# Soft-capped attention and soft mixture of experts on one core: polynomial exponentials on pairs of tiles

## The chip, the cores and the metric

The kernel runs on one core of one Trainium2 chip. The metric is the device time of one execution in microseconds; lower is better. The core has TensorE (PE) for matrix products, ScalarE (ACT) for tables such as exp and tanh, VectorE (DVE) for elementwise work, GpSimd (POOL) and SyncE (SP). In this kernel GpSimd casts v and issues the loads of weights, q and k; SP issues the loads of v and the stores of the output.

## What is computed

Attention over 8 batches of 12 heads, 448 tokens and head size 64, with scores capped by a tanh, and then a mixture of experts in which every token goes softly to 32 slots (8 experts with 4 slots each). Cut to what matters:

```python
scores = scale * np.matmul(q, k.transpose(0, 1, 3, 2))
scores = cap * np.tanh(scores / cap)
attn = np.exp(scores - max) / sum
x = np.matmul(attn, v)                      # then (3584, 768)

logits = x @ phi                            # 3584 x 32
d = softmax over tokens of logits
slot_input = d.T @ x                        # per expert 4 x 768
slot_out[e] = np.maximum(slot_input[e] @ w1[e], 0.0) @ w2[e]
out = softmax over slots of logits @ slot_out
```

cap is 30, so exp needs no subtraction of a maximum here; the kernel works without one.

## The kernel before

Two heads that lie beside each other in the array are a pair (48 pairs), two pairs a quad Q (24 quads, three to a batch of the input). A tile is 64 keys of both heads against 448 queries: 128 partitions by 448. Each pair has 7 tiles, 336 in all, and 6 tiles are a chunk j, 56 chunks. So one batch of the input is 7 chunks, and the main loop's pattern repeats every 7 chunks.

In chunk j ScalarE does two tanh over three tiles each (line 306, reading scores from PSUM) and one exponential over the tiles of chunk j-1 (line 310, in place). To relieve ScalarE, some tiles get their exponential on VectorE: poly_exp (lines 334 to 344) builds 2 to a power by a cubic polynomial in five steps. Step 0 scales to fixed point in int32 (line 337), step 1 shifts the whole part into the exponent of a bfloat16 (line 339), steps 2 to 4 are scalar-tensor-tensor instructions (lines 340 to 342) on the fraction. They use one work space, xe, xp and xb, of one tile's size. PARTS and EXTRA say for each chunk whether its first tile goes this way and in which slot of which chunk each step is issued; exp_chunk then leaves that tile out.

The order of every engine's queue is written by hand. The loop over j has slots named 0, e, a, b, r, c and d, between the fixed calls: tanh, exponential of the chunk before, the first part of a pair's product with v (pv_first), slot a, its tail, the scores of a coming half chunk (qk_chunk), slot b, the rest of the product and its normalisation (pv_rest with slot r, then norm: a reciprocal, line 367, and a multiplication, line 370), slot c, scores, slot d. A "<" or ">" puts a call at the start or end of a slot. WHEN places transposes of q and k, transposes of x, logits and sums; FILL places matmuls that compute nothing. A pair is normalised two chunks after its last tile.

PSUM is used in full: two buffers of three banks for scores (psS), one bank for the product (psV), one for all transposes and small sums (psT). So one slow reader in psV or psT holds PE up.

Other names that matter: vcast (272) casts a quad's v from vraw to one of two block-diagonal buffers vbd on GpSimd and then loads the next v. x_transp (415) turns one pair's x; logits (432) multiplies one quad's x with phi and adds the result into lg with VectorE; e_exp (448) takes the exponential of lg on ScalarE. wjobs (122) lists the loads of weights: w1, then the part of w2 that goes to DRAM as bfloat16 (w2d), then the part that stays (w2b, R2 blocks). After the attention, its pools are closed, and w2d is read back into the memory that they leave (w2t, lines 788 to 793). hpad, which holds the hidden layer with zeros around, takes the place of the work space.

## Time and profile before

| | |
|---|---|
| Median of 3 runs | 301.31 us (301.26 to 301.6) |
| The profiled execution | 301.64 us, span 299.9 us |
| ACT tanh, line 306 | 161.6 us busy, 113 instructions |
| ACT exponential, line 310 | 144.0 us busy, 58 instructions |
| DVE polynomial, lines 337, 339, 340, 341, 342 | 19.8, 18.2, 31.7, 33.6 and 29.9 us busy, 45 instructions each |
| DVE xT copies, line 419 | 17.9 us busy, 46 instructions |
| POOL casts of v, lines 275 and 276 | 21.7 and 25.3 us busy, 23 instructions each |
| PE fill, line 390 | 14.0 us busy, 244 instructions |
| w2t read back, line 792 | 20 transfers of 384 KB, 5.9 us to landing |
| Granted clock of TensorE | 0.988 of full, mean of the span |

The span is the time from the first to the last instruction of the profiled execution; the execution's own time is a little longer. Busy times of a row are sums of durations, and on ScalarE and VectorE the end of one instruction overlaps the start of the next, so starts are compared rather than durations where rates matter.

### The profile page before, as it was taken

What the parts mean: (1) busy time and instruction counts of PE and PEld (TensorE: products, weight loads), DVE (VectorE), ACT (ScalarE), POOL (GpSimd) and SP (SyncE); (2) the same over time, 40 slices, a digit from 0 to 9 for tenths busy, and PEclk for the clock granted to TensorE, in tenths of its full rate; (3) what the DMA queues carried; (4) which work ended last, traced back from release to release, by engine and by line L of the source; (5) the groups of instructions that cost most, each with busy time, mean ns of one, the idle gap of its engine ahead of it and who ended that gap; (6) DMA issues with size and microseconds to landing.
All of it is one profiled execution on the core that took longest, in us unless ns stands there. A gap on an engine that the chain in (4) does not pass through costs nothing.

```text
span 299.9 us, 10423 instructions
## 1 busy us (share of the span) xinstructions
PE 262.7 (88%) x4561; PEld 175.2 (58%) x4561; DVE 236.8 (79%) x511; ACT 268.0 (89%) x211; POOL 137.7 (46%) x179
## 2 busy tenths in 40 slices
PE   8898988998899989988998889998899999999830
PEld 7655656656665666565665666565666677642410
DVE  3728989888998999899988997999899974236850
ACT  3999999999999999999999999999999999136740
POOL 4493663395439525943393539453834232000000
PEclk9999999999999999999999999999999999999995
DMA  7999999699999999999989999999999749938997
GB/s 231 236 206 204 209 206 205 137 207 203 231 199 195 195 231 195 213 201 231 181 114 230 230 224 191 203 229 229 157 220 229 174 127 342 404 142 329 405 420 316
DMA packets 58061, 67.69 MB, mean 226 GB/s; under 512 B 3873, under 2 KB 54305, under 8 KB 58017
## 3 DMA queue, kind: packets, MB, share of 16 engines
q0 software_dynamic: 42448, 35.31, 76.2%
q1 hardware_dynamic: 15280, 31.50, 29.6%
q8 instruction: 35, 0.57, 0.7%
q10 hardware_dynamic: 288, 0.23, 0.3%
q14 instruction: 10, 0.07, 0.1%
HBM read 91.32 MB, written 18.87 MB: 367 GB/s over the span
## 4 chain that ended last, share of the span: by engine, by line
ACT 57%; PE 22%; DVE 13%; issue 3%; DMA 1%; POOL 1%; DVEq 0%; SPq 0%; ACTq 0%
ACT ex L306 32%; ACT ex L310 23%; PE pv L360 5%; PE sc L297 2%; DVE xq L370 2%; PE so_ps L843 2%; DVE ex L342 2%; PE hp L810 2%; DVE work L341 2%; DVE work L340 1%; ACT ob L935 1%; PE boot L618 1%; PE op L879 1%; PE op L926 1%; PE junk L615 1%
## 5 line engine op out<-in xcount | busy, mean ns | idle before, releaser
L306 ACT ACTIVATE ex<-sc 128x1344 bf16<-128x1344 f32 (+1 forms) x113 | 161.6, 1682 | 1.3 <-PE sc L297 1.3
L310 ACT ACTIVATE ex<-ex 128x2240 bf16<-128x2240 bf16 (+4 forms) x58 | 144.0, 2508 | 0.1
L360 PE MATMUL pv<-vbd,ex 128*128 128x130 bf16 (+1 forms) x1610 | 94.4, 211 | 10.6 <-DVE xq L370 5.5
L360 PEld LDWEIGHTS <-ex 128*128 128x128 bf16 (+1 forms) x1680 | 76.0, 101 | 31.6 <-issue 6.7
L297 PE MATMUL sc<-qT,kT 64*64 64x448 bf16 x672 | 69.8, 359 | 4.2 <-ACT ex L306 3.3
L275 POOL CAST vbd<-vraw 64x896 bf16<-64x896 f32 x23 | 21.7, 943 | 69.1 <-PE pv L360 40.9
L341 DVE SCALAR_TENSOR_TENSOR work<-work 128x448 f32<-128x448 f32 x45 | 33.6, 747 | 0.8
L456 POOL COPY e<-E 128x512 bf16<-128x512 bf16 x9 | 5.5, 613 | 60.0 <-ACT E L450 30.6
L340 DVE SCALAR_TENSOR_TENSOR work<-work 128x448 f32<-128x448 uint16 x45 | 31.7, 704 | 0.0
L297 PEld LDWEIGHTS <-kT 64*64 64x64 bf16 x672 | 24.7, 105 | 10.2 <-issue 6.8
L342 DVE SCALAR_TENSOR_TENSOR ex<-work 128x448 bf16<-128x448 f32 x45 | 29.9, 663 | 0.7
L370 DVE TENSOR_TENSOR xq<-pv,rec 128x448 bf16<-128x448 f32 x46 | 28.7, 624 | 1.6
L276 POOL CAST vbd<-vraw 64x896 bf16<-64x896 f32 x23 | 25.3, 1101 | 1.4
L115 POOL DMA_DIRECT2D w1b<-in_moe_w_dram x32 | 24.8, 777 | 0.0
L419 DVE COPY xT<-xps 128x448 bf16<-128x448 bf16 x46 | 17.9, 388 | 6.7 <-PE xps L413 6.2
L337 DVE TENSOR_SCALAR work<-ex 128x448 int32<-128x448 bf16 x45 | 19.8, 441 | 0.0
L267 DVE COPY kT<-kps 128x896 bf16<-128x896 bf16 x23 | 14.3, 622 | 6.3 <-PE kps L265 5.6
L339 DVE TENSOR_SCALAR work<-work 128x448 uint16<-128x448 uint16 x45 | 18.2, 404 | 0.5
L187 POOL DMA_DIRECT2D kb<-in_k_dram x22 | 16.1, 732 | 5.3 <-PE kps L265 4.7
L187 POOL DMA_DIRECT2D qb<-in_q_dram x22 | 16.2, 734 | 3.0 <-DMA kraw<-in_k_dram 3.0
L408 PE MATMUL xps<-ident,xq 128*128 128x128 bf16 x141 | 15.5, 219 | 1.7 <-DVE slacc L511 1.4
L367 DVE RECIPROCAL rec<-pv 128x7 f32<-128x7 f32 x46 | 9.3, 203 | 9.4 <-PE pv L360 8.8
(136 smaller groups left out, 346.3 us busy)
## 6 DMA issues: line engine op xcount, KB each, us to landing
w1b<-in_moe_w_dram POOLq DMA_DIRECT2D x32, 384.0 KB, 8.9
vraw<-in_v_dram SPq DMA_DIRECT2D x23, 448.0 KB, 6.2
w2d<-in_moe_w_dram POOLq DMA_DIRECT2D x20, 384.0 KB, 9.7
w2t<-w2d SPq DMA_DIRECT2D x20, 384.0 KB, 5.9
out_dram<-ob SPq DMA_DIRECT2D x7, 768.0 KB, 6.7
qb<-in_q_dram POOLq DMA_DIRECT2D x22, 224.0 KB, 9.2
kb<-in_k_dram POOLq DMA_DIRECT2D x22, 224.0 KB, 8.5
w2b<-in_moe_w_dram POOLq DMA_DIRECT2D x12, 384.0 KB, 8.8
```

The costliest lines, as they stand in the source:

```text
L115: pool.dma_start(out=w1b[e][:, js, fs], in_=w1r[:, e, js, fs])
L187: (sp if nm == "v" else pool).dma_start(out=t, in_=quad_ap(nm, Q))
L275: pool.tensor_copy(t[0:HP, :, :, 0:DH], raw[0:HP])
L276: pool.tensor_copy(t[HP:P, :, :, DH + 1:VW - 1], raw[HP:P])
L297: pe.matmul(sc[cs, u, 0:S], qkT["k", Q][r, c, cs], qkT["q", Q][r, :, cs], start=True, stop=True)
L306: act.activation(exs[j][:, half * CS + u0:half * CS + u1, :], sc[:, u0:u1, 0:S], ACT.Tanh, scale=qk_scale / cap)
L310: act.activation(exs[j][:, u0:u1, :], exs[j][:, u0:u1, :], ACT.Exp, scale=cap)
L340: lambda: dve.scalar_tensor_tensor(xp, frac, p2, frac, ALU.add, ALU.mult),
L341: lambda: dve.scalar_tensor_tensor(xp, xp, p1, frac, ALU.add, ALU.mult),
L342: lambda: dve.scalar_tensor_tensor(t, xp, p0, xb, ALU.add, ALU.mult))
L360: pe.matmul(out_, exs[j][r, u, q0:q0 + (HP if tail else P)], v_, start=(c == 0 and g == gs[0] < NF), stop=(c == NT - 1), skip_group_check= ...
L370: dve.tensor_tensor(xq[Q][:, h, s0:s1, :], pv[:, 0:s1 - s0, 0:DH], rec.to_broadcast([P, s1 - s0, DH]), op=ALU.mult)
```

## The change

The polynomial works on one or two tiles at once. The work space doubles, and xe, xp and xb are cut to the size that a call needs. In chunks 7 to 48, every second residue modulo 7 (0, 2, 4 and 6) now gives its first two tiles to VectorE; chunks 3 to 5 and 50 to 53 give one as before, chunks 6 and 49 none. All placings in PARTS, WHEN and FILL are new.

x is turned by quads with one copy instead of by pairs with two. The logits of a batch are formed in one go over all six parts in PSUM, and the small exponential reads them there; lg is gone, and the call moves to a new slot m between the two tanh. In the last batch the sum that identity matmuls brought in is formed by products directly.

v is loaded and cast in halves of 64 partitions. A half-cast follows directly after a pair's products; where the buffer itself would not make it wait, a memset of one element that is already zero does. 10 parts of w2 (of 4 blocks by half the columns) stay instead of 12, 22 go through DRAM instead of 20. The pools of the attention are laid out in the order in which they die, and hpad moves into the memory that they leave. Three of the first junk matmuls go.

```diff
-    R2 = 24
+    KEPT = 10
...
-    w2b = wts.tile([P, R2, D], BF16, name="w2b")
+    w2b = wts.tile([P, KEPT, 4, HD], BF16, name="w2b")
...
+    w2_parts = [(n0, half) for n0 in range(0, len(blocks), 4) for half in range(2)]
+    w2_kept, w2_spilled = w2_parts[:KEPT], w2_parts[KEPT:]
...
-    work = consts.tile([P, 5 * S // 2], I32, name="work", tag="work", bufs=1)
-    xe, xp, xb = work[:, 0:S], work[:, S:2 * S].bitcast(F32), work[:, 2 * S:].bitcast(BF16)
...
-    for nm in ("ex1", "ex2", "vb0", "ex3", "ex4", "ex0", "vb1"):
...
+    NP = 2
+    for nm in ("qk0", "ex1", "wk", "ldv", "ex2", "ex3", "vb0", "qk1", "ex4", "ex0", "vb1"):
+        homes[nm] = att.enter_context(tc.tile_pool(name=nm, bufs=1))
...
+    work = wk.tile([P, 5 * NP * S // 2], I32, name="work")
+    xe, xp = work[:, 0:NP * S], work[:, NP * S:2 * NP * S].bitcast(F32)
+    xb = work[:, 2 * NP * S:].bitcast(BF16)
...
+    vraw = ldv.tile([P, 2, S], F32, name="vraw")
+
+    def load_v(Q, n):
+
+        if Q < NQ:
+            r = slice(n * HP, n * HP + HP)
+            src = quad_ap("v", Q)
+            sp.dma_start(out=vraw[r],
+                         in_=bass.AP(tensor=src.tensor, offset=src.offset + n * S * DH,
+                                     ap=[[NT * DH, HP]] + list(src.ap[1:])))
+            raws["v", Q] = vraw
...
-    def vcast(Q):
-        raw = raws.pop(("v", Q)).rearrange("p h (c d) -> p h c d", d=DH)
-        t = vbds[Q % 2]
-        pool.tensor_copy(t[0:HP, :, :, 0:DH], raw[0:HP])
-        pool.tensor_copy(t[HP:P, :, :, DH + 1:VW - 1], raw[HP:P])
+    def vcast(Q, n):
+        raw = raws["v", Q].rearrange("p h (c d) -> p h c d", d=DH)
+        r, c0 = slice(n * HP, n * HP + HP), n * W
+        pool.tensor_copy(vbds[Q % 2][r, :, :, c0:c0 + DH], raw[r])
         if Q != 1:
-            load("v", max(Q + 1, 2))
+            load_v(max(Q + 1, 2), n)
+
+    def vcast_after(pr):
+
+        Q, h = divmod(pr, 2)
+        if h == 0 and 1 < Q + 1 < NQ:
+            pool.memset(vbds[Q % 2][HP:P, h, NT - 1, 0:1], 0.0)
+            vcast(Q + 1, 1)
+        elif h == 1 and Q + 2 < NQ:
+            vcast(Q + 2, 0)
...
+    PARTS = {0: (2, ((0, "a", (0,)), (1, "a", (1, 2)), (1, "c", (3,)), (1, ">d", (4,)))),
+             2: (2, ((0, "a", (0,)), (0, ">d", (1, 2)), (1, "a", (3,)), (2, "a", (4,)))),
+             4: (2, ((0, "a", (0,)), (0, ">b", (1,)), (0, ">d", (2,)), (1, "<b", (3,)), (1, ">d", (4,)))),
+             6: (2, ((0, "r", (0, 1)), (0, "<d", (2,)), (0, ">d", (3,)), (1, "<d", (4,))))}
+    shared = {j: (PARTS[j % 7],) for j in range(7, NCH - 8) if j % 7 in PARTS}
...
-    def poly_exp(j, u, ops):
-        t = exs[j][:, u, :]
+    def poly_exp(j, u, tiles, ops):
+        n1 = tiles * S
+        t = exs[j][:, u:u + tiles, :].rearrange("p u s -> p (u s)")
+        e, p, b = xe[:, 0:n1], xp[:, 0:n1], xb[:, 0:n1]
+        f, w = frac[:, 0:n1], whole[:, 0:n1]
...
-    def x_transp(pr, copy=dve.tensor_copy):
...
+    def x_transp(Q, hs=(0, 1), copy=dve.tensor_copy):
+        if Q not in xTs:
+            xTs[Q] = xs.tile([P, 2, S], BF16, name="xT", tag="xT", bufs=3)
+        ps = psT.tile([P, 2, S], BF16, name="xps", tag="T")
+        for h in hs:
+            turn_x(ps[:, h, :], 0, 2 * Q + h, range(NG))
+        copy(xTs[Q][:, hs[0]:hs[-1] + 1, :], ps[:, hs[0]:hs[-1] + 1, :])
...
-    def logits(Q, ps=None):
...
+    def logits(b):
+        lps[b] = psT.tile([P, NG, NS], F32, name="lps", tag="T")
         for g in range(NG):
...
+            for jt in range(NJ):
+                phi_mms(lps[b][:, g, :], xTs[b * NQB + jt // 2][:, jt % 2, :], g, jt,
+                        jt == 0, jt == NJ - 1)
...
-        act.activation(es[b], lgs.pop(b), ACT.Exp)
+        act.activation(es[b], lps.pop(b), ACT.Exp)
...
-    FILL = ((3, "a", fill, 2), (4, "a", fill, 2), (5, "a", fill, 2), (6, "a", spare, 10), (6, "c", spare, 12), (7, "a", fill, 18), (8, "a", fill, 8), (9, "a", fill, 2))
+    FILL = ((3, "a", fill, 16), (4, "a", fill, 10), (5, "a", fill, 8), (6, "a", spare, 10), (6, "c", spare, 14), (7, "a", fill, 12), (8, "a", fill, 16), (9, "a", fill, 4))
...
+    WHEN = {"k1": (0, "a"), "q1": (-1, "d"), "v1": (1, "c"), "k2": (2, "b"), "q2": (2, "d"), "v2": (4, "b"), "k3": (4, "b"), "q3": (5, "b"), "v3": (10, "b"), "x0": (5, "a"), "x1": (8, "d"), "x2": (10, "a"), "lg": (10, "d"), "ee": (11, "m"), "ss": (11, "d"), "et": (13, "a"), "en": (13, "b"), "es": (14, "c")}
...
-    busy(28)
+    busy(25)
...
         tanh_chunk(2 * j)
         if j == NCH - 1:
             exp_chunk(j - 1)
+        run(j, "m")
         tanh_chunk(2 * j + 1)
...
             pv_rest(pr, aux.pop((j, "r"), ()))
+            vcast_after(pr)
...
-    for s in range(2):
-        pe.matmul(lps[s], id32s[0], lg[:, 2 * s:2 * s + 2, :], start=True, stop=False,
-                  skip_group_check=True)
-    x_transp(last - 2)
+    x_transp(NQ - 2, (1,))
...
     for gs in ((0, 1, 2), (NF,)):
-        for pr in (last - 3, last - 2):
+        for pr in range(last - 5, last - 1):
             phi_last(pr, gs)
...
-    clear_hpad()
...
+    for n0, half in sorted(w2_spilled, key=lambda x: (x[1], x[0])):
+        t = tl.tile([P, 4, HD], BF16, name=f"w2t{n0}_{half}")
+        sp.dma_start(out=t, in_=w2d[n0, half])
+        w2t[n0, half] = t
+
+    hpad = tl.tile([P, E, NFT, NS], BF16, name="hpad")
+    pool.memset(hpad, 0.0)
```

## The prediction

> **What bounds the kernel now.** I read the page's shares first, then the chain, then the groups by shape, then the same five stretches for all engines, and last the timelines of ScalarE and VectorE inside one stretch. The page's first part and its chain:

> ```profile
> PE 262.7 (88%) x4561; PEld 175.2 (58%) x4561; DVE 236.8 (79%) x511; ACT 268.0 (89%) x211; POOL 137.7 (46%) x179
> ...
> ACT 57%; PE 22%; DVE 13%; issue 3%; DMA 1%; POOL 1%; DVEq 0%; SPq 0%; ACTq 0%
> ```

> Three engines are near 80 to 90%, so the mean does not decide. The main loop repeats every 7 chunks (one batch), and the exponential over all six tiles comes once in a batch, so its starts mark the period: 60.97, 91.77, 122.57, 153.37, 184.17 in the chain. That is 30.80 us each time. Busy times of the engines in these stretches:

> ```profile
> 60.97:91.77 30.80, 28.04 (x518) 19.16 (x516) 27.73 (x60) 30.80 (x23) 18.19 (x24) 1.00 1.15 207
> 91.77:122.57 30.80, 28.45 (x531) 19.59 (x528) 28.17 (x62) 30.80 (x23) 18.06 (x24) 1.00 1.16 205
> 122.57:153.37 30.80, 28.19 (x520) 19.32 (x519) 27.78 (x62) 30.80 (x24) 16.70 (x22) 1.00 1.12 196
> 153.37:184.17 30.80, 27.48 (x519) 19.04 (x519) 27.59 (x61) 30.80 (x24) 17.29 (x22) 1.00 1.20 206
> 184.17:214.97 30.80, 27.13 (x514) 18.86 (x511) 28.38 (x59) 30.80 (x24) 18.01 (x23) 1.00 1.20 208
> ```

> After the length come PE, weight loads, VectorE, ScalarE, GpSimd. ScalarE is busy in the whole of every stretch: it is the bound, with PE (mean 27.86) and VectorE (about 27.9) only 2.9 us behind. What ScalarE does there, with its starts:

> ```profile
> 122.02 2.88 ACT L310 ACTIVATE ex<-ex 128x2688 bf16<-128x2688 bf16 x1
> 124.36 2.91 ACT L306 ACTIVATE ex<-sc 128x1344 bf16<-128x1344 f32 x2
> 126.69 2.53 ACT L310 ACTIVATE ex<-ex 128x2240 bf16<-128x2240 bf16 x1
> 128.66 2.93 ACT L306 ACTIVATE ex<-sc 128x1344 bf16<-128x1344 f32 x2
> 131.00 2.54 ACT L310 ACTIVATE ex<-ex 128x2240 bf16<-128x2240 bf16 x1
> ```

> From start to start, six tiles of exponential cost 2.34 us, five 1.97, two tanh 2.34; durations are longer because neighbours overlap. One tile is worth 0.373 us of ScalarE. VectorE and GpSimd beside it:

> ```profile
> 133.21 0.62 DVE L340 SCALAR_TENSOR_TENSOR work<-work 128x448 f32<-128x448 uint16 x1
> 133.86 1.25 DVE L341 SCALAR_TENSOR_TENSOR work<-work 128x448 f32<-128x448 f32 x1
> 135.15 0.62 DVE L342 SCALAR_TENSOR_TENSOR ex<-work 128x448 bf16<-128x448 f32 x1
> ...
> 133.41 1.23 POOL L276 CAST vbd<-vraw 64x896 bf16<-64x896 f32 x1
> ```

> The same instruction that usually takes 0.62 us took 1.25 while a cast of v ran on GpSimd.

> [...] the closest starts in the timeline are 0.53 to 0.54 for the scalar-tensor-tensor steps and 0.29 to 0.30 for the tensor-scalar ones[...]

> **The change part by part.**

> *ScalarE.* Before, 45 tiles go to the polynomial (chunks 3 to 6, 36 in chunks 7 to 48, chunk 49, chunks 50 to 53). After, 3 in chunks 3 to 5, none in 6 and 49, 48 in chunks 7 to 48, 4 in 50 to 53: 55. Each of the six batches from 7 to 48 loses two tiles on ScalarE, 0.75 us, a floor of 30.05; chunks 6 and 49 gain one each. 10 x 0.373 = 3.73 us less in all. The seven small exponentials stay; their source becomes PSUM, 0.2 us start to start now, taken as unchanged.

> *VectorE.* One single-tile polynomial is two steps of 0.30 and three of 0.54: 2.22 us. [...] Per batch: 6 x 2.22 = 13.3 becomes 4 x 4.03 = 16.1, plus 2.8. The copies of x go from 6 x 0.30 to 3 x 0.54, minus 0.2; the copy and two sums of lg (0.19 + 2 x 0.20) go, minus 0.6. The other work (k and q copies, 6 x 0.77 of norm, small ones) stays, about 8.6. The clean sum goes from 24.25 to 26.25.

> To that comes stretch. Adding up starts in 60.97 to 184.17 (four batches) gives 114.0 us, 28.5 per batch, with 2.3 idle. So 4.25 is stretch: about 1.8 from cast collisions (steps beside casts against those not), the rest the 0.1 us between dependent steps and unevenness. After, 20 dependent steps replace 30, about 1.5 to 1.8. The casts are now released when a pair's products are done, just when VectorE does the reciprocal and the scaling (0.77 us, PSUM in, no collision), so I take 1.2 for them, between 0.5 and 1.8. VectorE then needs 26.25 + 1.6 + 1.2 = 29.05 per batch.

> *PE.* Fill goes from 34 to 66 matmuls a batch; 18 of them take 0.65 us with a first of 0.19, so 0.027 each: plus 0.87. Two more short junk matmuls: 0.1. Transposes, logits and products keep their number. 27.86 becomes 28.85. Its waits for v (2.6 us in four batches) should go, as half-casts come a pair or more ahead.

> *GpSimd, SP, transfers.* As many casts (64 partitions each, 0.93 us), 22 one-element memsets at about 0.1, which make the queue wait for a pair's products. Weight, q and k loads are queued behind that wait; the queue already stands idle 40.9 us for those products. The v loads become twice as many of half the size on SP. Two more parts of w2 are written to DRAM and read back (22 against 20 at 384 KB), about 1 us each of SP's train; the first half's read-back has had time since 237 while PE first uses it at 266.4. Nothing on the path. If that cover were gone, 2 us.

> *Head and tail.* Three junk matmuls less before the first transposes: 3 x 0.11 = 0.33, of which I take 0.2, because VectorE's cast of k ends at 4.08 and the transposes started at 4.28. At the end four identity matmuls (0.6) go and two more pairs of logits (0.4) come: zero. The clearing of hpad (1.8 us) moves behind the closing of the pools; the last reads of x end near 258.9 and hpad is written first after 263.5, so 2 us of slack hide it.

> *The new wait on ScalarE.* The small exponential now waits between two tanh for all six logits, with any later tanh behind it. PE can begin them after the score chunk before it, 0.57 us, and needs 3 x 0.42; ScalarE has a 1.59 exponential and a 1.17 tanh to do first: 2.76 against about 2.2. I take zero; without that half microsecond it is up to 0.5 x 7 = 3.5 us.

> *Sum.* A floor of 30.05, VectorE at 29.05 and PE at 28.85 need an almost perfect fit; each waits for the other two within one or two chunks (two score buffers, one product bank, one transpose bank), and a pair step of 0.99 can stand in front of a norm. Bounds on the period: 30.05, and 26.25 + 4.25 + 0.7 (a third of VectorE's idle kept) = 31.2. I take 30.3. Then six batches give 6 x -0.50 = -3.0, chunks 6 and 49 give +0.75, the head -0.2: -2.45. The profiled execution took 301.64 (span 299.9, 1.7 around it) and would take 299.2; the median of the runs is 0.33 lower, 301.31, so 298.9.

> **Rivals.** (1) ScalarE keeps its floor: 6 x -0.75 + 0.75 - 0.2 = -3.9, 297.4. For it: ScalarE had no gap in five batches with the others at 91%. Against: they would be at 96 to 97%. (2) VectorE and PE eat the gain: period 30.7, no change, about 301.2. (3) Slower: VectorE's order becomes the bound. Pair steps keep the cast collisions at 1.8 or raise them (a cast caught by three steps of 0.99 instead of 0.54), norms come late, the one product bank is freed late, the next scores come late and ScalarE gets gaps. At a period of 31.1 this is 6 x 0.3 + 0.75 - 0.2 = +2.35, 303.7. It decides from a period of 30.71 on, that is when VectorE's stretch and idle together exceed 4.46 us a batch; they are 6.55 now. For it: near 200 to 245 VectorE already carries the chain. Against: part of that idle is only VectorE being early.

> **How the numbers follow.** Forecast (period 30.1 to 30.65, 297.7 to 300.7) 0.42; ScalarE's floor kept (rival 1) 0.15, a third of it under 297.3; no change 0.09; slower 0.34, a third of it over 303.6. Faster by over 0.2% (0.6 us, what a measurement of this kernel can tell from none): 0.42 + 0.15 = 0.57; within it 0.09; slower 0.34. The range from 297.3 to 303.6 leaves out 0.05 and 0.11; the forecast's own is 297.7 to 300.3.

> **What would show it.** 24 exponentials of 1792, 7 of 2240 and 24 of 2688 elements; pair steps starting 0.53 and 0.99 apart; the period between ScalarE's marks, 30.05 to 30.5 if right, over 30.7 if the third rival holds, with ScalarE idle before tanh (scores late) or before the small exponential. Steps beside casts back at 0.1 to 0.3 of delay show the casts right. A read-back or hpad waited for after 260 would make the tail wrong.

## The result, and the profile after

The changed kernel took 302.25 us (median of 4 runs, 301.81 to 302.71), the kernel before 301.46 beside it: ratio 1.0026, 95% interval 1.0007 to 1.0044. Forecast were 298.9 us and a gain of 2.4; it became a loss of 0.8. A second set, of 22 runs of the changed kernel, gave 302.68 against 301.41 (1.0051, 1.0033 to 1.0069).

The profiled execution took 301.81 us, 0.17 more than that of the kernel before, with the same span of 299.9. Its first part and its chain:

```profile
PE 266.3 (89%) x4820; PEld 179.9 (60%) x4820; DVE 231.4 (77%) x397; ACT 264.9 (88%) x211; POOL 137.3 (46%) x200
...
ACT 52%; PE 25%; DVE 9%; issue 5%; POOL 3%; DMA 2%; DVEq 0%; ACTq 0%; POOLq 0%
```

ScalarE's busy sum is 3.1 us smaller, VectorE has 114 instructions fewer, PE 259 matmuls more (mostly filler, the matmuls that compute nothing). The exponentials by shape, of ScalarE's groups, are the ones that the change asks for (24, 24 and 7):

```profile
L324 ACT ACTIVATE ex<-sc 128x1344 bf16<-128x1344 f32 x111 | 142.2, 1355 | 0.6 <-PE sc L315 0.6
L328 ACT ACTIVATE ex<-ex 128x2688 bf16<-128x2688 bf16 x24 | 60.0, 2502 | 0.1
L328 ACT ACTIVATE ex<-ex 128x1792 bf16<-128x1792 bf16 x24 | 42.7, 1778 | 0.0
L328 ACT ACTIVATE ex<-ex 128x2240 bf16<-128x2240 bf16 x7 | 15.0, 2140 | 0.0
```

Between one small exponential E and the next lies one batch. Five of them (start and end, length, then busy time of PE, weight loads, VectorE, ScalarE, GpSimd, the granted clock of TensorE, the DMA share and GB/s):

```profile
54.80:84.84 30.04, 28.06 (x547) 19.45 (x545) 27.45 (x45) 30.04 (x23) 17.97 (x25) 1.00 1.17 208
84.84:115.18 30.34, 28.89 (x562) 20.28 (x561) 28.33 (x46) 30.28 (x23) 17.71 (x25) 1.00 1.17 209
115.18:145.43 30.25, 28.45 (x555) 19.90 (x553) 28.17 (x45) 30.20 (x23) 16.85 (x24) 1.00 1.22 211
145.43:176.10 30.67, 28.82 (x562) 20.20 (x560) 28.48 (x46) 30.24 (x23) 17.66 (x25) 1.00 1.18 202
176.10:206.57 30.47, 28.44 (x555) 19.89 (x553) 27.91 (x45) 30.24 (x22) 18.00 (x25) 1.00 1.21 206
```

The mean is 30.35 us a batch, as forecast (30.3), and the loop's last tanh starts at 248.42 instead of 250.54: 2.12 us are won up to there. The first layer of the experts starts 1.82 us earlier (257.58 for 259.40), and so does everything up to the last result that VectorE writes (286.75 for 288.57). Yet the last packet of the output lands at 298.38 instead of 298.31. The whole gain goes between the issue of the first store and the last packet. This stretch of the kernel before, and then of the changed kernel, in the same columns:

```profile
269.49:298.31 28.82, 15.92 (x126) 6.35 (x125) 15.82 (x24) 13.84 (x20) 0.61 (x1) 0.90 0.97 382
```

```profile
267.67:298.38 30.71, 15.92 (x126) 6.35 (x125) 15.82 (x24) 13.83 (x20) 0.61 (x1) 0.83 0.94 359
```

The engines do the same work in both, to 0.01 us, and are idle for half of it. What is full is the last column but one, the share of the DMA engines: 0.97 and 0.94. The stores (11.0 MB) went at 382 GB/s and then at 359, and so need 1.89 us more. The timelines of SP's queue, first before and then after, show one place:

```profile
269.49 0.81 SPq L876 DMA_DIRECT2D out_dram<-obh  x2
270.40 1.85 SPq L859 DMA_DIRECT2D out_dram<-obh  x4
```

```profile
267.67 1.45 SPq L885 DMA_DIRECT2D out_dram<-obh  x2
269.22 1.86 SPq L868 DMA_DIRECT2D out_dram<-obh  x4
```

The first two issues take 1.45 us instead of 0.81, though the profile shows nothing that they wait for. And the store packets themselves are longer: those of 1536 bytes 67.2 ns in the mean instead of 64.8, those of 6144 bytes 240.6 instead of 234.6.

### The profile page after: what moved, and what is told of

Read it like the earlier page. It is cut to its first block, busy times and chain, and to the rows that moved or that the text cites. A ratio compares the mean times of both kernels' runs of the same rounds, so it can differ in the third digit from the quotient of the medians.

```text
span 299.9 us, 10895 instructions
## 1 busy us (share of the span) xinstructions
PE 266.3 (89%) x4820; PEld 179.9 (60%) x4820; DVE 231.4 (77%) x397; ACT 264.9 (88%) x211; POOL 137.3 (46%) x200
## 3 DMA queue, kind: packets, MB, share of 16 engines
q1 hardware_dynamic: 15920, 32.28, 31.1%
## 4 chain that ended last, share of the span: by engine, by line
ACT 52%; PE 25%; DVE 9%; issue 5%; POOL 3%; DMA 2%; DVEq 0%; ACTq 0%; POOLq 0%
ACT ex L324 28%; ACT ex L328 22%; PE pv L381 7%; PE sc L315 3%; PE so_ps L852 2%; PE hp L819 2%; DVE xq L391 1%; POOL vbd L285 1%; DVE ex L363 1%; DVE work L362 1%; PE xps L429 1%; ACT ob L944 1%; PE op L888 1%; PE pv L411 1%; DMA qraw<-in_q_dram 1%
## 5 line engine op out<-in xcount | busy, mean ns | idle before, releaser
L324 ACT ACTIVATE ex<-sc 128x1344 bf16<-128x1344 f32 (+1 forms) x113 | 143.5, 1344 | 1.8 <-PE sc L315 1.8
L328 ACT ACTIVATE ex<-ex 128x2688 bf16<-128x2688 bf16 (+5 forms) x58 | 120.5, 2085 | 0.1
L363 DVE SCALAR_TENSOR_TENSOR ex<-work 128x896 bf16<-128x896 f32 (+1 forms) x31 | 31.3, 1009 | 0.2
L362 DVE SCALAR_TENSOR_TENSOR work<-work 128x896 f32<-128x896 f32 (+1 forms) x31 | 30.2, 974 | 0.1
L361 DVE SCALAR_TENSOR_TENSOR work<-work 128x896 f32<-128x896 uint16 (+1 forms) x31 | 30.2, 973 | 0.0
L360 DVE TENSOR_SCALAR work<-work 128x896 uint16<-128x896 uint16 (+1 forms) x31 | 20.6, 665 | 0.4
L358 DVE TENSOR_SCALAR work<-ex 128x896 int32<-128x896 bf16 (+1 forms) x31 | 20.6, 665 | 0.1
L411 PE MATMUL pv<-ones 128*128 128x57 bf16 x496 | 20.6, 188 | 0.0
L411 PEld LDWEIGHTS <-ones 128*128 128x128 bf16 x496 | 17.4, 96 | 0.3
L119 POOL DMA_DIRECT2D w2d<-in_moe_w_dram x22 | 16.8, 786 | 0.0
```

Source lines behind the costliest of these rows:

```text
L324: act.activation(exs[j][:, half * CS + u0:half * CS + u1, :], sc[:, u0:u1, 0:S], ACT.Tanh, scale=qk_scale / cap)
L328: act.activation(exs[j][:, u0:u1, :], exs[j][:, u0:u1, :], ACT.Exp, scale=cap)
L358: lambda: dve.tensor_scalar(e, t, cap * math.log2(math.e) * FRAC, (127 + math.log2(lead)) * FRAC, ALU.mult, ALU.add),
L361: lambda: dve.scalar_tensor_tensor(p, f, p2, f, ALU.add, ALU.mult),
L362: lambda: dve.scalar_tensor_tensor(p, p, p1, f, ALU.add, ALU.mult),
L363: lambda: dve.scalar_tensor_tensor(t, p, p0, b, ALU.add, ALU.mult))
```

## The experiments

**The changed kernel again**, unchanged, in more runs. Theory A lays the longer packets to where the buffers of the stores now begin.

> The changed kernel as it is, once more. In its first profile ScalarE's last tanh came 2.1 us sooner than before, layer 1 1.8 us sooner, and the end not at all: the stores took 30.1 us instead of 28.4, with packets of 1536 bytes at 67 ns instead of 65 and of 6144 bytes at 240 instead of 234. Both theories expect the same of the loop again (layer 1 starts near 257.7). Theory A [...] expects 66 to 68 and 240 ns again; theory B (the slower packets were chance of one execution, the end is fixed by something else) expects other packet times, 65 and 234 among them. Time 0.2 to 0.4% above before.

302.68 us, ratio 1.0051 [1.0033, 1.0069]; 31.05 us from the first store's issue to the last packet. The loss is real, and rather larger than in the first four runs.

**128 bytes of padding.** The change moves `work` (4480 bytes a partition) out of the pool that lies ahead of the weights, and 4480 is 35 times 128: all buffers allocated after it, those of the stores among them, move by an odd multiple of 128 bytes (worked out from the sizes; the traces show no addresses). The pad of 128 bytes makes the move an even multiple in the changed kernel, and an odd one in the kernel before. That this would matter was the author's guess:

```diff
+    consts.tile([P, 32], F32, name="pad")
```

> The changed kernel with 128 bytes per partition of unused memory ahead of the weight pool[...]. Theory A: packets at 65 and 234 ns, the stores 0.8 to 1.7 us shorter, the time 300.5 to 301.4, that is 0.8 to 1.7 us under the changed kernel. Theory B: the time of the changed kernel within 0.3 us, about 302.2.

> The kernel before with the same 128 bytes, so that its buffers now start 128 bytes off. Theory A: packets at 67 and 240 ns and 0.8 to 1.7 us more than before, 302.2 to 303.1. Theory B: no change, within 0.3 us of 301.4.

The changed kernel with the pad took 301.14 us (ratio 0.9993, 0.9979 to 1.0007), 1.54 less than without beside it; the kernel before with the pad 302.19 (1.0024, 1.0015 to 1.0032), 0.78 more. The packets follow: 64.9 and 234.8 ns in the first, 67.6 and 240.3 in the second. The store phases of the kernel before with the pad, and of the changed one with it:

```profile
269.46:299.03 29.57, 15.91 (x126) 6.35 (x125) 15.82 (x24) 13.85 (x20) 0.61 (x1) 0.87 0.97 372
```

```profile
267.44:297.30 29.86, 15.91 (x126) 6.35 (x125) 15.82 (x24) 13.85 (x20) 0.61 (x1) 0.89 0.94 369
```

In the first the share is still 0.97 but GB/s are fewer: the engines are as full and each packet costs more. In the second the packets are as short as before the change and the share has the gap of the changed kernel: something else is lost there, 1.04 us (29.86 for 28.82). The size of the effect is 2.4% on packets of 6144 bytes (240.3 ns for 234.6) and 0.75 us on this phase (29.57 for 28.82). Why a move of 128 bytes lengthens packets was not shown.

**The old filler.** The counts of junk matmuls that keep PE busy go back to those of the kernel before, 266 matmuls fewer; the pad stays.

```diff
-    FILL = ((3, "a", fill, 16), (4, "a", fill, 10), (5, "a", fill, 8), (6, "a", spare, 10), (6, "c", spare, 14), (7, "a", fill, 12), (8, "a", fill, 16), (9, "a", fill, 4))
+    FILL = ((3, "a", fill, 2), (4, "a", fill, 2), (5, "a", fill, 2), (6, "a", spare, 10), (6, "c", spare, 12), (7, "a", fill, 18), (8, "a", fill, 8), (9, "a", fill, 2))
```

> The padded changed kernel with the fill counts of the kernel before: 34 instead of 66 short matmuls that compute nothing in each batch. Theory A (PE has room, the fill lies in its idle time, the period of 30.35 us comes from waits for norms and scores): period and time within 0.3 us of the padded one, 301.1. Theory B (PE at 95% holds the period above ScalarE's floor of 30.05): 0.87 us of PE less per batch takes the period to 30.05 to 30.15, the time 1.2 to 1.8 us down, near 299.6.

The median says nothing happened: 301.58 us, ratio 0.9997 [0.9978, 1.0015]. But the 22 runs are spread from 299.1 to 303.5, and the loop of the profiled one is of two kinds. Three batches of it:

```profile
114.44:144.34 29.90, 27.96 (x521) 19.06 (x519) 27.82 (x45) 29.90 (x24) 16.99 (x24) 1.00 1.21 212
144.34:177.13 32.79, 29.30 (x523) 20.23 (x521) 28.05 (x46) 30.94 (x23) 17.67 (x25) 0.95 1.13 188
177.13:207.05 29.92, 28.11 (x530) 19.44 (x528) 28.02 (x45) 29.92 (x23) 18.15 (x25) 1.00 1.21 210
```

Four of five batches go at 29.9 us; one takes 32.79. Inside that one, a wait of PE and then three windows, the last of them over the 3.41 us ahead of the drop of the clock:

```profile
PE qps L276 <- DMA qb<-in_q_dram: 2.1, 1, 2.1
```

```profile
156.00:158.20 2.20, 0.14 (x4) 0.02 (x2) 1.59 (x2) 2.20 (x3) 0.14 (x1) 1.00 1.26 237
158.20:162.00 3.80, 3.80 (x64) 3.45 (x67) 1.64 (x3) 3.09 (x3) 0.00 (x0) 0.56 1.29 210
155.21:158.62 3.41, 1.35 (x23) 0.59 (x21) 2.34 (x3) 3.41 (x3) 0.93 (x2) 1.00 1.25 236
```

PE stands 2.1 us for the queries `qb`, and is then granted half its clock for 3.41 us, in which ScalarE runs dry (3.09 of 3.80). In the 3.41 us ahead of the drop PE was busy for 1.35. The runs' own clocks fit: the four at 299.1 to 299.6 us had a mean of 0.983 to 0.986, the other 18 of 0.972 to 0.981.

**Narrow junk.** The padded kernel with one spare filler issued as ten matmuls of 128 columns instead of 3 of 384 and one, so that PE has 84 more instructions and the same multiplying. By the traces, PE's instructions arrive as DMA packets of 16 KB on a queue of their own, one for about 130 matmuls (35 packets for 4561 matmuls before, 37 for 4820 after); this is the fetch spoken of from here on, and its moment shifts with the number of instructions (8 matmuls more took it from 0.60 us after the first store to 0.42 ahead of it, in two runs below).

```diff
-    FILL = (... (6, "a", spare, 10), ...)
+    FILL = (... (6, "a", spare, 10, 1), ...)
```

> The padded changed kernel with the ten-unit junk of each batch issued as ten short matmuls instead of three long and one short: the same PE time, 84 PE instructions more ahead of the tail. In the three profiles of the changed kernel a 16 KB instruction fetch lies over the second store's issue, which takes 0.9 to 1.35 us; in the two of the kernel before the fetch was over by then and the issue took 0.38. Theory A [...]: the fetch comes 84 instructions sooner, before the first store, the second store's issue takes 0.4, the time falls 0.5 us to about 300.6. Theory B (the read-backs or the number of transfers on the queue make it slow): the issue stays at 0.9 or more and the time at 301.1.

301.68 us, 1.0021 [1.0006, 1.0037]. The gain that was hoped for did not come. The trace says why: the fetch of instructions moved ahead of the first store, as it should (it begins 2.06 us before it), and the second store's issue is short again (none of the first eight over 0.42 us). But the fetch after it now comes 9.7 us into the stores, and one store's issue there takes 1.57 us; the phase is 30.39 us. Moving one fetch out ahead of the stores brought the next one in among them.

**Single tiles again.** The padded kernel with the single-tile polynomials of the kernel before, in their old slots.

```diff
-    PARTS = {0: (2, ((0, "a", (0,)), (1, "a", (1, 2)), (1, "c", (3,)), (1, ">d", (4,)))),
...
+    PARTS = {0: ((0, "a", (0,)), (0, "<b", (1,)), (0, "c", (2,)), (0, "<d", (3,)), (0, ">d", (4,))),
...
```

> The padded changed kernel with the polynomial of the kernel before: 45 single tiles in the old slots, everything else of the change kept. Theory A (the pairs alone make the loop shorter): the period back at 30.6 to 30.8, ScalarE's last tanh 2 us later than in the padded kernel, the time 302.6 to 303.3. Theory B (the other parts carry the gain, the direct logits and the early casts): last tanh less than 0.7 us later, time under 301.8.

325.65 us, 1.0796 [1.0753, 1.0838]: far from what either theory gave. Two batches, and ScalarE's waits in the loop:

```profile
57.73:91.68 33.95, 29.57 (x554) 20.95 (x553) 27.00 (x55) 31.00 (x23) 17.95 (x25) 0.95 1.07 187
91.68:125.74 34.06, 30.06 (x562) 21.35 (x561) 27.11 (x57) 31.14 (x22) 17.98 (x25) 0.95 1.07 183
```

```profile
ACT ex L325 <- PE sc L316: 12.0, 9, 2.2
ACT E L471 <- PE lps L455: 4.8, 6, 0.8
```

VectorE is busy for only 27 of 34 us, and still ScalarE gets scores and logits late: PE waits 9.0 us for copies of k and 7.0 for norms. That these stand in VectorE's queue behind polynomial steps placed for another order is the likely reason; it was not tried apart. And each of the two batches also holds a stretch of 3.41 us at half the clock (0.95 in the mean). So the run doesn't price the pairs: the order of the transposes and the slots of the polynomial belong together and can't be undone singly. It shows a loop 3.5 us a batch longer than that of the padded kernel with no engine full.

The run also shows that standing alone does not bring the half clock. PE stands for 1.3 to 1.7 us twelve times in this loop; six of these stands are followed by it and six are not. In the clock records of all profiles, the changes lie whole multiples of 3.41 us apart. Within the loops, a stretch of this grid with PE busy for under half of it was always followed by half clock, one with over 0.67 of it never, and between 0.53 and 0.67 both happened. So where a stand falls on the grid, which differs from one execution to the next, has a part in it.

**Queries earlier.** With the old filler, the load of queries that PE waits for has to be earlier (quad_in(Q, ...) in the code issues the loads of quad Q+1). The first attempt moved one that is not it; the second of these two also has 8 short matmuls more at the loop's end, to shift the fetch.

```diff
-            quad_in(3 * b + 1, (j - 1, "b"), (j, "a"), ...
+            quad_in(3 * b + 1, (j - 2, "d"), (j - 1, "b"), ...
...
-    for j, slot, n in ((NCH - 6, "d", 8), (NCH - 4, "d", 8), (NCH - 2, "d", 12)):
-        at(j, slot, spare, n)
+    for j, slot, n, *k in ((NCH - 6, "d", 8, 1), (NCH - 4, "d", 8, 1), (NCH - 2, "d", 12)):
+        at(j, slot, spare, n, *k)
```

> The changed kernel with the 128-byte pad and the old filler counts (as in the run with the old filler), and the load of each batch's first following quad issued one to two chunks earlier: keys at (j-2, d) instead of (j-1, b), queries at (j-1, b) instead of (j, a). In the run with the old filler alone the loop went at 29.9 us a batch, ScalarE's own need, but for one batch of 32.8, in which TensorE stood 2.1 us for qb and was then granted half its clock for 4 us; four of its 22 runs, at a mean clock of .983 to .986, took 299.1 to 299.6. Theory (the filler that the change added pays for a late query transfer, .45 us a batch, and is not needed once the transfer is early): TensorE's waits for qb in the loop under 0.5 us, all batches within 29.8 to 30.7, mean clock .983 or more, median 299.0 to 299.7, ratio .992 to .995. Rival (the old filler is too little for the clock wherever TensorE waits): the clock dips elsewhere, mean .972 to .981, median 301.0 to 302. Neither theory expects over 302.5.

> The kernel with the early query load, with two tail fillers of 8 issued as narrow matmuls, 8 matmuls (16 TensorE instructions) more, so that the 16 KB instruction fetch comes some 0.6 us earlier against the first stores: at 267.4 as in the padded run (129 matmuls before the end) instead of 0.7 us after the first store. Theory [...]: the second store's issue .9 to 1.0 us instead of 1.8, from the first store's issue to the last packet 29.8 to 30.0 instead of 30.7 us, median 0.5 to 0.9 below the run beside it. Rival [...]: the same time as the run beside it within 0.2 us.

300.91 us (0.9968, 0.9952 to 0.9984) and 300.62 (0.9957, 0.9940 to 0.9974). The half clock was still there, in the fifth batch of both profiles (32.2 us), and in the first also near 43 us, so the first expectation fell, and the rival seemed to hold. Which load it was came out of GpSimd's timeline, here of the run with the old filler:

```profile
146.82 1.51 POOL L120 DMA_DIRECT2D w2d<-in_moe_w_dram  x2
148.21 1.06 POOL L286 CAST vbd<-vraw 64x896 bf16<-64x896 f32 x1
149.09 0.83 POOL L186 DMA_DIRECT2D qb<-in_q_dram  x1
```

It is the load of the quad before that (3b+4, counted from the batch before), issued at 149.09 behind two weight copies (one in the batch before) and a cast; PE uses it at 158.18, after its wait. The question of the fetch was answered: in the first it begins 0.60 us after the first store and the phase takes 29.55 us, in the second 0.42 us before it, and the phase takes what it took in the kernel before:

```profile
266.63:295.46 28.83, 15.91 (x126) 6.35 (x125) 15.82 (x24) 13.84 (x20) 0.61 (x1) 0.85 0.97 382
```

The medians differ by 0.3 us only, within the spread of two loops that both lose their clock at times.

**The right load.** The loads of quad 3b+4 come earlier in place of those of 3b+2: its queries are now issued ahead of the weight copies of their chunk. With the old filler and the shift, and with the filler of the change.

```diff
-        quad_in(3 * b + 3, (j + 4, "a"), (j + 5, "a"), when("k3"), when("q3"), when("v3"))
+        quad_in(3 * b + 3, (j + 3, "c"), (j + 4, "a"), when("k3"), when("q3"), when("v3"))
```

> As the run with the early query load and the shifted fetch, but with the other load moved: the two runs before moved the load that comes second in a batch, while the one that TensorE waited for is the last (quad 3b+4, queries issued at (j+5, a), used in (j+6, d)). It now goes at (j+4, a), ahead of the weight copies w2d of its chunk, and its keys at (j+3, c); the load moved before is back in its place. In the profiles with the old filler the fifth batch issues two copies of w2d ahead of it instead of one, it lands some 8.5 to 9 us after its issue instead of 7.3, and TensorE stands 1.5 to 2.1 us, whereupon the granted clock is half for 3.4 us. Theory (that load is what the filler of the change covers): no wait for qb, no stretch at half clock in the loop, mean clock .985 or more, each batch 29.9 (the sixth 30.6), median 298.2 to 299.2, ratio .989 to .992. Rival (the filler is needed wherever the old one leaves TensorE idle, for instance at 43 us in the run before): half clock in another batch in most executions, median 300 to 301.

> The padded changed kernel with the filler of the change and the same load early. Theory (the added filler itself costs the loop .45 us a batch, as TensorE's work is then what ends last in it): no gain, batches 29.9 to 30.8 as in the padded run, median 300.7 to 301.3, ratio .998 to 1.0. Rival (what costs the loop is not the filler but the late query transfer): the loop at 29.9 us a batch, median 298.5 to 299.5.

With the old filler: 298.63 us, ratio 0.9919 [0.9893, 0.9946], the fastest of all, and 0.3 us below the time that was forecast for the change itself. Its loop, the same five batches:

```profile
54.92:84.80 29.88, 27.89 (x519) 19.02 (x517) 27.91 (x45) 29.88 (x23) 17.95 (x25) 1.00 1.17 206
84.80:114.69 29.89, 28.28 (x526) 19.32 (x524) 27.90 (x46) 29.89 (x24) 17.88 (x25) 1.00 1.19 211
114.69:144.57 29.88, 27.95 (x521) 19.05 (x519) 27.81 (x45) 29.88 (x23) 16.82 (x25) 1.00 1.22 212
144.57:174.46 29.89, 28.21 (x527) 19.28 (x525) 28.20 (x46) 29.89 (x23) 17.44 (x26) 1.00 1.20 203
174.46:204.35 29.89, 27.86 (x519) 18.96 (x517) 27.73 (x45) 29.89 (x24) 17.55 (x26) 1.00 1.24 211
```

ScalarE's column equals the length in every line: this is its floor, and the clock is 1.00 throughout. With the filler of the change: 300.56 us, 0.9980 [0.9961, 0.9999]; its five batches took 29.89, 30.45, 30.24, 30.61 and 30.23 us. So the filler costs 0.4 us a batch, and what it bought was cover for one late transfer: it holds PE back. In the padded kernel PE asks for the fifth batch's queries at 157.59 and stands 0.50 us for them, with the old filler it asks at 156.12 and stands 2.06; they are there at 158.1 to 158.2 in both.

Where the time shows in the changed kernel: ScalarE's timeline near 154 and 175 us, and then the fastest kernel's.

```profile
153.03 1.31 ACT L324 ACTIVATE ex<-sc 128x1344 bf16<-128x1344 f32 x1
154.73 1.29 ACT L324 ACTIVATE ex<-sc 128x1344 bf16<-128x1344 f32 x1 [0.39 <-PE sc L315]
...
174.70 1.35 ACT L324 ACTIVATE ex<-sc 128x1344 bf16<-128x1344 f32 x1
176.10 0.28 ACT L467 ACTIVATE E<-lps 128x128 bf16<-128x128 f32 x1
```

```profile
152.16 3.08 ACT L325 ACTIVATE ex<-sc 128x1344 bf16<-128x1344 f32 x2
154.50 3.07 ACT L329 ACTIVATE ex<-ex 128x2688 bf16<-128x2688 bf16 x1
156.84 3.10 ACT L325 ACTIVATE ex<-sc 128x1344 bf16<-128x1344 f32 x2
```

Two tanh take 2.34 us from start to start in the fastest (154.50 - 152.16), so one takes 1.17. In the changed kernel one is late by 0.53 us (1.70 for 1.17), and the small exponential by 0.23 (1.40 for 1.17): after the first batch, scores and logits come late at such places once or twice in a batch.

**The fetch alone, in the kernel before.** Its spare fillers as narrow matmuls, 98 more, so that a fetch falls among its first stores.

```diff
-    FILL = (... (6, "a", spare, 10), (6, "c", spare, 12), ...)
+    FILL = (... (6, "a", spare, 10, 1), (6, "c", spare, 12, 1), ...)
```

> The kernel before, with its two spare fillers of each batch (10 and 12) issued as narrow matmuls: 98 matmuls more, the same multiplying in the same slots. TensorE then fetches its last 16 KB of instructions some 106 matmuls before its end instead of 136, so at about 0.1 us after the issue of the first store instead of 1.35 us before it. Nothing else of the store phase changes. Theory (a fetch among the first stores makes the last packet late): second store's issue 0.9 to 1.8 us instead of .38, first store's issue to last packet 29.4 to 29.9 instead of 28.8 us, loop as before (30.7 a batch), median 0.5 to 1.0 above the kernel before, ratio 1.0015 to 1.0035. Rival (the 0.7 us between the two runs with the early loads came from elsewhere): store phase 28.8, ratio .999 to 1.001.

302.39 us against 301.41, ratio 1.0039 [1.0023, 1.0056]; the profiled execution took 303.22, so that its phase shows more than the median does. The loop is as before (30.67 a batch), the fetch came 1.5 us after the first store (0.1 was expected), and the fourth store's issue took 1.97 us. SP's queue, and the phase:

```profile
269.67 0.81 SPq L876 DMA_DIRECT2D out_dram<-obh  x2
270.59 3.45 SPq L859 DMA_DIRECT2D out_dram<-obh  x4
```

```profile
269.67:299.88 30.21, 15.92 (x126) 6.36 (x125) 15.82 (x24) 13.84 (x20) 0.61 (x1) 0.89 0.93 365
```

Four issues in 3.45 us, for 1.85 in the kernel before, and 1.39 us more for the phase. The profiles together, without that of the single tiles, from the packets of the traces (one execution each; times in us; the beginning of the fetch counts from the issue of the first store; off: the buffers lie an odd multiple of 128 bytes from where those of the kernel before do):

| kernel | fetch begins | it takes | first store to last packet |
|---|---|---|---|
| before | -1.34 | 0.96 | 28.8 |
| old filler, earlier queries (3b+2), shifted | -0.42 | 0.93 | 28.8 |
| changed, padded | -0.04 | 1.03 | 29.9 |
| changed, padded, earlier queries (3b+4) | -0.10 | 0.96 | 29.7 |
| the fastest | -0.17 | 1.20 | 29.9 |
| old filler, earlier queries (3b+2) | +0.60 | 1.23 | 29.6 |
| old filler | +0.69 | 1.65 | 30.7 |
| before, narrow junk | +1.48 | 1.53 | 30.2 |
| narrow junk | -2.06 and +9.73 | 0.93, 1.30 | 30.4 |
| before, with the pad (off) | -1.16 | 1.31 | 29.6 |
| changed (off) | +0.12 | 0.96 | 30.7 |
| changed, second profile (off) | +0.11 | 1.31 | 31.1 |

In the kernels not marked off, the phase takes 28.8 us where no fetch begins later than 0.42 us ahead of the first store, and 29.6 to 30.7 where one begins from 0.17 ahead on. The second row has all of the change but its filler, and its 28.8 speaks against the other parts, the two further read-backs of w2 among them.

## Why the prediction was wrong

*The loop came out, partly by luck.* Its period is 30.35 for 30.3, VectorE's need 28.6 for 29.05 (30.35 less 8.7 us of waits in five batches), the head -0.2 as taken. The pair steps with three operands take 1.00 to 1.07 us from start to start where 0.99 was taken; the other two take 0.67 to 0.77 in the mean for 0.53, some of them beside casts and GpSimd's issues. The 4.03 us of a pair in the sum were the author's estimate, which no trace of the kernel before shows; in the changed kernel the closest starts are 0.53 us apart for the two steps and 1.00 for the three, 4.06 in all. The reciprocal and the scaling take 0.20 and 0.62 us beside casts as they do alone, in both kernels. The four-tile exponential was put at 1.59 us, which is 2.34 less two tiles of 0.373, and takes 1.59 from start to start. Up to the last tanh 2.12 us were won for 2.45.

But the period before was read wrongly. It came from the chain, whose pieces begin where the piece before ends; they slide away from the starts, because these exponentials overlap the next instruction by more and more. The chain of the kernel before, and its timeline of the same two exponentials:

```profile
122.57 2.33 ACT ex L310
153.37 2.33 ACT ex L310
```

```profile
122.02 2.88 ACT L310 ACTIVATE ex<-ex 128x2688 bf16<-128x2688 bf16 x1
152.70 3.01 ACT L310 ACTIVATE ex<-ex 128x2688 bf16<-128x2688 bf16 x1
```

From start to start the period was 30.68 there and 30.67 in the mean of five, not 30.80. So the floor was 29.92, not 30.05, and a period of 30.3 was worth 0.37 a batch and not 0.50: 1.7 us by the same sum. Of the 2.12 won, 0.33 come from one late tanh in the sixth batch of the kernel before (217.88). And 30.3 was a choice between bounds of 30.05 and 31.2. Two smaller sums don't come out either: a period of 30.65 gives 301.0 and not 300.7 as the end of the forecast's range, and 0.57 with 3 x 0.42 is 1.83, not 2.2.

The reason given, that VectorE and PE would be too full for ScalarE to keep its floor, was only half right. The first rival was possible: at nearly the same load on VectorE (27.9 us a batch for 28.1) the fastest kernel keeps its floor, 29.89. What held the changed kernel above it was its filler: priced at 0.87 us of PE beside ScalarE's work, it cost 0.4 us a batch on the path, as the two kernels with the right load early show.

*The step that failed* is "Nothing on the path" for the transfers, and with it the sum, which carried what the loop wins unchanged to the end. It asked of the transfers after the loop only whether they come in time, and looked at the read-back and hpad; both were in time. The stage that sets the end is the stores, bound by the DMA engines (a share of 0.97 before), and the change touched it in two ways that the diff shows only indirectly. Its buffers moved by an odd multiple of 128 bytes: +0.75 us. PE's count of instructions changed, and with it the moment of its last fetch, from 1.34 us ahead of the first store to 0.12 after it: +1.04, the padded kernel against the kernel before. The two make 1.79 of the 1.89 us, from single profiles. Each was put into the kernel before alone and made that slower, by 0.78 us and by 0.98 in the medians (there with the fetch at +1.48).

*The end of the loop* lost 0.3 us: "zero" for the tail set four identity matmuls against two more pairs of logits, but without the former PE stands 0.34 us for VectorE's norm at 249.5, ahead of the transposes, a wait that they had covered, and the latter come on top (0.21 us more).

*The profiled executions and the medians.* The profiles leave 0.17 us between the kernels, the medians 0.8; the second profile of the changed kernel (302.66, with a phase of 31.05) is nearer to its median. How long the fetch takes among the stores varies from 0.96 to 1.65 us in the table.

*Smaller steps.* The waits of PE for v did not go: 4.1 us in 9 places over the loop for 3.5 in 7. PE's waits in the loop, before and after:

```profile
PE pv L360 <- POOL vbd L275: 3.5, 7, 0.7
```

```profile
PE pv L381 <- POOL vbd L285: 4.1, 9, 0.7
```

The half-casts come earlier, but the last of each quad still waits for the pair whose buffer it takes. The wait of the small exponential, taken as zero with 3.5 us as its bound, cost 0.15 to 0.27 us in five batches of the changed kernel and nothing in the fastest, where PE is ahead. The third rival, VectorE's order, did not happen in the change; the run with single tiles looks like it, with the half clock mixed in.

*Open.* What the fetch takes from the stores was not shown (the traces give a packet's queue, not its engine); nor why the padding gained 1.54 us in the changed kernel but cost 0.78 in the kernel before. By the profiles 0.2 to 0.4 us of the gain lie ahead of the stores, whose first is issued at 267.44 with the pad and at 267.67 and 267.88 without, and 0.8 to 1.2 in the phase. Six of the 22 later runs of the changed kernel took over 304 us, with no lower granted clock than the others; none of them was profiled. A kernel with the fastest loop and the fetch clear of the stores, some 1 us better by the table, was not run. The fastest stands on 6 runs, one of them at 301.02.

## What to carry to other kernels

A gain in a loop counts only as far as the stage that ends last lets it through: if that stage is bound by the DMA engines, ask of every change what it does to the addresses of that stage's buffers and to what else uses those engines then, even where none of its lines is touched. Read a period from the starts of one instruction in the timeline, not from the pieces of a chain. Filler matmuls can be hiding a late transfer (here PE stood 0.50 us for it with them and 2.06 without); look at what PE waits for where the filler is taken out, move that load, and the filler's time may come free. A median that doesn't move can be two effects of opposite sign: the spread of the runs and a table by batch showed it here.
